# Attention decode kernel: K of the last pair in one load, and `wo` in six loads instead of seven

## The chip, the cores and the metric

The kernel runs on one core of a Trainium2 chip. The metric is the device time of one execution in microseconds (us). The core has four compute engines that matter here: TensorE (PE in the profile, with its weight loads as PEld), VectorE (DVE), ScalarE (ACT) and GpSimd (POOL). SyncE (SP) issues the loads; its queue is called SPq. Each engine runs its own program in order, and the programs meet only at semaphores.

## The reference

One decoding step of attention over a large cache, times a gate from a small MLP:

```python
# x (2,1,512); k_cache, v_cache (2,32,8192,128); wq (512,4096); wo (4096,512), all float32
xn = layernorm(x)
q = heads(xn @ wq)                                  # 2 x 32 heads, 1 query, 128 wide
scores = einsum("bhqd,bhkd->bhqk", q, k_cache) * 128 ** -0.5
o = einsum("bhqk,bhkd->bhqd", softmax(scores), v_cache)
s = merge_heads(o) @ wo
g = silu(mlp(layernorm(xn)))                        # w1, b1, gelu, w2, b2
return x + s * g
```

The two caches are 268 MB each, so nearly all bytes that the kernel reads are K and V, and every one is read once.

## The kernel before, in words

**Tiling.** There are 2 x 32 = 64 heads. A tile is the K (or V) of two heads: partitions 0 to 63 hold one head and 64 to 127 the other, 128 rows of 128 numbers in each partition, 8.4 MB in all. So there are N = 32 K tiles and 32 V tiles, numbered 0 to 31 here (K0 to K31, V0 to V31), and a *pair* is two tiles, K(2i) and K(2i+1). SBUF holds three such tiles: `KBUF[0]` and `KBUF[1]` take the K tiles in turn, and `VB` takes every V tile but the last. V31 goes to `KBUF[0]`, so that `wo` (8.4 MB too, 32 rows of 512 columns in each partition) can go to `VB`. In the profile all three buffers are called `big`.

**VectorE** works on each K tile in two long instructions: a multiplication with the query (`tensor_tensor`, in place) and a sum over the 128 numbers of a row (`tensor_reduce`, into `sc`). Then it takes the maximum (`MX`), waits for TensorE to transpose that, and reduces it to the negative maximum of each head (`nm`). The function is `scores` (line 317). The first 15 pairs run in a hardware loop (line 331); the last pair, K30 and K31, is written out behind the loop (lines 335 to 337). K31 is loaded in two halves on two semaphores, `d_k1` and `d_kl`, and `scores` multiplies and sums one half and then the other.

**TensorE** runs a loop of 31 turns (line 492): `weighted` multiplies the softmax weights `PZ` with a V tile (64 matmul instructions), transposes the result by way of `o`, and frees `VB` (`p_free`); `softmax` transposes the maximum, spreads the bias, and frees the K buffer (`p_k`). Between these it does matmuls of `Q` with `ident` whose results nobody reads (`unread`, line 448): they only keep TensorE occupied. `unread(4, 4)` stands ahead of the wait for the maximum, `unread(4, 2)` ahead of V31, `unread(2)` between the halves of V31, and a few short ones behind it.

**ScalarE** computes the exponentials into `PZ`, and copies TensorE's sums to SBUF.

**The end** (lines 501 to 530): when V31 has been weighted, VectorE spreads the result (`Z`), TensorE sums it, and VectorE divides by the softmax sums, which gives `on`, the attention output. TensorE then multiplies `on` with the 32 rows of `wo`, in order of the rows, and waits for each load of `wo` by its semaphore `d_wo0`, `d_wo1` and so on. Rows 0 to 27 make one sum in bank 1 (`pw`), which ScalarE copies (`wide`, into `o`); rows 28 to 31 and that copy are added up in `acc`; VectorE multiplies with the gate and adds x (`res`), and SyncE stores it.

**The order of the loads.** SyncE issues, in this order: ..., K31 (waits for `p_k` of tile 29), V30 (waits for `p_free` of tile 29), V31 in two halves (waits for `p_k` of tile 30), then all loads of `wo` (wait for `p_free` of tile 30), and after all work the store. The loads of one queue move their data in the order of issue.

Of the kernel before, what the change touches and what calls it, by code (L numbers as in the profile page):

```python
# [5 lines left out]
ALU = mybir.AluOpType  # L6
AX = mybir.AxisListType
# [6 lines left out]
class Program:  # L14
# [28 lines left out]
    def take(self, eng, name, v=1):  # L43

        self.engines[eng].wait_ge(self.sem(name), v).then_inc(self.sem(name), -v)  # L45

    def op(self, eng, method, *args, waits=(), sig=None, by=1, quiet=False, **kwargs):
        need = self.need(eng, waits)
        for name, v in need[:-1]:
            self.engines[eng].wait_ge(self.sem(name), v)  # L50
        ins = getattr(self.engines[eng], method)(*args, **kwargs)  # L51
        for name, v in need[-1:]:
            ins._wait_ge(self.sem(name), v)
        if quiet:
            return None
        name = sig or "own_" + eng
        by = 16 if method == "dma_start" else by
        ins.then_inc(self.sem(name), by)
        self.counts[name] += by
        return name, self.counts[name]  # L60


def decode_kernel(nc, x, kc, vc, wq, wo, w1, b1, w2, b2, out):
    P = 128
    B, H, S, DH = kc.shape
# [3 lines left out]
    U = 2  # L69
    HP = P // U  # L70
    KP = S // HP
    HH = H // U
    N = B * HH
# [13 lines left out]
    OC = DH // PH  # L87
    BH = B * H
    NPB = 512 // DH
    WO_CUTS = (0, 10, 18, 24, 28, 30, 31, 32)  # L90
    WIDE = 28
    HALVES = (0, KP // 2, KP)

    pr = Program(nc)
    op, wait, take = pr.op, pr.wait, pr.take

    def sb(shape, name):
        return nc.alloc_sbuf_tensor(name, list(shape), F32).ap()
# [4 lines left out]
    kf = kc.rearrange("b h s d -> (b h s d)").rearrange("(n p j d) -> n p j d", p=P, j=KP, d=DH)  # L103
# [4 lines left out]
    KBUF, VB = rows[:2], rows[2]  # L108
# [24 lines left out]
    Q = sb([P, N, DH], "Q")  # L133
# [21 lines left out]
    SC = [sb([P, KP], f"sc{i}") for i in range(2)]  # L155
# [36 lines left out]
    def pe_n(name, n):  # L192
        return name, n + 1
# [9 lines left out]
    op("SP", "dma_start", wq_sb, wq.rearrange("(p c) n -> p c n", p=P), sig="d_wq")  # L203

    def load_k(n, *waits):
        sems, cuts = ([f"d_k{n % U}", "d_kl"], HALVES) if n == N - 1 else ([f"d_k{n % U}"], (0, KP))
        for name, (c0, c1) in zip(sems, zip(cuts, cuts[1:])):
            op("SP", "dma_start", KBUF[n % U][:, c0:c1], kf[n][:, c0:c1], sig=name, waits=waits)

    load_k(0)  # L210
    t["w2"] = op("SP", "dma_start", w2_sb[:, :NF, :], w2[:NF * P, :].rearrange("(p c) n -> p c n", p=P), sig="d_w2")

# [13 lines left out]
    for k in (7, 6, 1, 2, 4, 0):  # L226
# [13 lines left out]
                  op=ALU.add)  # L240
    t["sel"] = op("DVE", "tensor_copy",
                  sel[:, HP:].rearrange("p (b j r) -> p b j r", b=B, r=HG)[:, :, :QT, 0], by_row[:, :B, :],
                  waits=[t["sel0"]])
# [36 lines left out]
    for part, n0, n1 in (("first", 0, NPB), ("rest", NPB, N)):  # L280
        shape = [BH, n1 - n0, DH]
        t[f"QN {part}"] = op("DVE", "tensor_tensor", out=QN[:, n0:n1, :], in0=q_all.unsqueeze(1).to_broadcast(shape),
                           in1=mine[:, n0:n1].unsqueeze(2).to_broadcast(shape), op=ALU.mult,
                           waits=[t["qall"], t["mine"]])
# [10 lines left out]


    load_k(1, pe("pq"), ("d_wq", 16))
    for b in range(B):
        t["x4"] = op("SP", "dma_start", x4[HB * b::R, :], x[b, 0].rearrange("(j n) -> j n", n=P), sig="d_x4",
                     waits=[t["x4m"]])  # L300
# [4 lines left out]
    for n in range(N - 2):  # L305
        load_k(n + 2, pe_n("p_k", n))
        op("SP", "dma_start", VB, vf[n + 1], sig="d_v", waits=[pe_n("p_free", n)])
# [4 lines left out]
    wo_v = wo.rearrange("(p c) n -> p c n", p=P)  # L312
    for i, (c0, c1) in enumerate(zip(WO_CUTS, WO_CUTS[1:])):
        op("SP", "dma_start", wo_sb[:, c0:c1], wo_v[:, c0:c1], sig=f"d_wo{i}")


    def scores(u, q, sems, cuts):
        k = KBUF[u]
        for name, (c0, c1) in zip(sems, zip(cuts, cuts[1:])):
            take("DVE", name, 16)  # L320
            op("DVE", "tensor_tensor", out=k[:, c0:c1], in0=k[:, c0:c1],
               in1=q.unsqueeze(1).to_broadcast([P, c1 - c0, DH]), op=ALU.mult, sig="v_t")
            take("DVE", "v_t")
            op("DVE", "tensor_reduce", out=SC[u][:, c0:c1], in_=k[:, c0:c1], axis=AX.X, op=ALU.add, sig="v_r")
        take("DVE", "v_r", len(sems))
        op("DVE", "tensor_reduce", out=MX, in_=SC[u], axis=AX.X, op=ALU.max, sig="v_mx")
        take("DVE", "p_m")
        op("DVE", "tensor_reduce", out=nm, in_=pm[:1, :P].rearrange("o (s r) -> o s r", s=U), axis=AX.X,
           op=ALU.max, negate=True, sig="v_nm")

    with nc.vector.Fori(0, N // U - 1) as i:
        take("DVE", "s_q")
        for u in range(U):
            scores(u, Q.rearrange("p (i u) d -> p i u d", u=U)[:, i, u, :], [f"d_k{u}"], (0, KP))
    take("DVE", "s_q")
    scores(0, Q[:, N - U, :], ["d_k0"], (0, KP))
    scores(1, Q[:, N - 1, :], ["d_k1", "d_kl"], HALVES)


    with nc.scalar.Fori(0, N // U) as i:  # L340
        for u in range(U):
# [4 lines left out]
            for s in range(U):  # L346
# [10 lines left out]
                   waits=[t["th"], t["pool"]])  # L357
    shape = [P, N, U * PH]
    t["ZL"] = op("DVE", "tensor_tensor", out=ZL, in0=half.unsqueeze(1).to_broadcast(shape),
                 in1=RS.unsqueeze(2).to_broadcast(shape), op=ALU.mult, waits=[pe_n("p_z", 0), t["half"]])  # L360
# [3 lines left out]
                in1=OT.unsqueeze(2).to_broadcast(shape), op=ALU.mult, waits=[t["OT"], t["blk"]])  # L364
    t["on"] = op("DVE", "tensor_tensor", out=on[:, ::HB, :], in0=OA[:, :, :OC], in1=rl.unsqueeze(2).to_broadcast([P, B, OC]),
                 op=ALU.mult, waits=[t["rl"], t["on0"], pe_n("p_oa", 0)])
    t["wide"] = op("ACT", "copy", o4, pw, waits=[pe_n("p_w", 0)])
    a = op("DVE", "scalar_tensor_tensor", res, acc, 0.5, gate, op0=ALU.mult, op1=ALU.mult,
           waits=[pe_n("p_acc", 0), t["gate"]])
    t["res"] = op("DVE", "tensor_add", res, res, x4, waits=[a, t["x4"]])  # L370
    t["out"] = op("SP", "dma_start", out.rearrange("b s (j n) -> j (b s) n", n=P), res[::HB, :], sig="d_out",
                  waits=[t["res"]])
# [27 lines left out]
    for c in range(ND):  # L400
# [4 lines left out]
        j, k = NF % QT, NF // QT  # L405
# [6 lines left out]
    j, k = NF % QT, NF // QT  # L412
    mm(ph[R * j:R * j + B, k * P:k * P + FT], ones[:1, :B], b1_sb[:, NF * P:], start=False, stop=True, sig="ph")
    by_tile = ident.rearrange("p (j r) -> p j r", r=R)
    for k in range(NH):
        n = min(QT, NF + 1 - k * QT)
# [9 lines left out]
    for n in range(NG // QT):  # L426
        for hh in range(HG):
# [3 lines left out]
               waits=[t["sel"], t["qnat"]], sig="pqa" if last else None)  # L431

    for g in range(N // NPB):
        mm(PB[g % len(PB)], sides, QN[:, g * NPB:(g + 1) * NPB, :].rearrange("h n d -> h (n d)"),
           waits=[t["side"], t["QN rest" if g else "QN first"]] + ([t[f"Q{QH}"]] if g >= len(PB) else []),
           sig=f"pb{g}")
    for f in range(NF + 1):
        j = f % QT
        k = P if f < NF else FT
        mm(pg[R * j:R * j + B, :], hT[:k, f, :], w2_sb[:k, f, :], start=f < QT, stop=f + QT > NF and j != QT - 1,  # L440
           waits=[t["hT"], t["w2"], t["mem6"]])
    mm(pg[R * (QT - 1):R * (QT - 1) + B, :], ones[:1, :B], b2_sb, start=False, stop=True, waits=[t["b2"]], sig="pg")
    for j in range(QT):
        mm(pgate[R * j:R * j + MB, :], mod_b[:, :MB], g_nat[:, j * P:(j + 1) * P], waits=[t["g"], t["mod_b"]],
           sig="pgate" if j == QT - 1 else None)
    assert done == PE_EVENTS, done

    def unread(*heads):

        for n in heads:  # L450
            mm(bank[6][:, :n * DH], ident, Q[:, :n, :].rearrange("p n d -> p (n d)"), waits=[t["g"], t[f"Q{QH}"]])
# [58 lines left out]
    for b in range(B):  # L510
        h = slice(b * H, (b + 1) * H)
        mm(OA[:, b, :OC], Z[:, h].rearrange("p h r -> p (h r)"), mod, waits=[t["Z"]],
           sig="p_oa" if b == B - 1 else None)
    unread(1)
    for i, (c0, c1) in enumerate(zip(WO_CUTS, WO_CUTS[1:])):
        for c in range(c0, c1):
            after = [t["on"], t["mem"], (f"d_wo{i}", 16)]
            if c < WIDE:
                j = c % QT
                mm(pw[R * j:R * j + MB, :], on[:, :, c], wo_sb[:, c, :], start=c < QT, stop=c + QT >= WIDE,  # L520
                   waits=after, sig="p_w" if c == WIDE - 1 else None)
# [5 lines left out]
        if c1 == OC - 2:  # L527
            for j in range(QT):
                mm(acc[R * j:R * j + MB, :], mod[:, :MB], o4[:, j * P:(j + 1) * P], start=False, stop=False,
                   waits=[t["wide"]])  # L530
# [26 lines left out]
```

## Time and profile before

| what | us |
|---|---|
| median of 3 runs (1299.6 to 1299.94) | 1299.65 |
| span of the profiled execution, first to last instruction | 1298.1 |
| what lies around the span, if that execution took the median | 1.55 |
| TensorE busy in the span | 466.2 |
| VectorE busy in the span | 1135.7 |
| ScalarE busy in the span | 72.0 |
| share of the DMA engines' time taken by the load queue | 99.7% |
| data read | 559.30 MB, 431 GB/s over the span |

The profile is one execution. Its page gives shares of the whole span; its timeline gives the start and the duration of each instruction (or of several alike, merged, with "xN"), and in brackets how long the engine had been idle and what ended that. `DVEq`, `PEq` and `ACTq` there are the engines' own sequencers: an instruction that waited for a semaphore ahead of the work is put down to them. `PEclk` is TensorE's granted clock, 1.00 for full and 0.50 for half.

### The profile page before, as it was taken

The page shows a single profiled execution, that of the slowest core. Times are in us where ns is not written, and L with a number is a line of the kernel's source. Part 1 is how long each engine was busy: PE and PEld are TensorE (multiplying, and loading weights), DVE is VectorE, ACT ScalarE, POOL GpSimd, SP SyncE. Part 2 cuts the span into 40 slices and gives each one's busy share as a digit, 9 for nine tenths or more (in the row PEclk, how much of TensorE's full clock was granted, in tenths as well). Part 3 has the DMA queues.
Part 4 walks back from the last instruction along what each step waited for, and adds up shares of the span by engine and source line. Part 5 has one row for each costly group of instructions (what it writes and reads, how often), then busy time and mean ns, then how long its engine had stood idle before and what let it go on. Part 6 is the DMA issues. An engine that isn't in the chain of part 4 may idle for free. (4 is left out here: it accounts for less than half of the span.)

```text
span 1298.1 us, 7183 instructions
## 1 busy us (share of the span) xinstructions
PE 466.2 (36%) x2958; PEld 151.0 (12%) x2958; DVE 1135.7 (87%) x171; ACT 72.0 (6%) x245; POOL 2.1 (0%) x14
## 2 busy tenths in 40 slices
PE   3813343323334322433322343322334321333338
PEld 1201111001111000111100111100111100111103
DVE  2599999988889988889988888988888988888991
ACT  1100000000000000000000000000000000000000
POOL 0000000000000000000000000000000000000000
PEclk8757766666776566677656767656776666677659
DMA  9999999999999999999999999999999999999998
GB/s 412 432 430 440 432 434 432 426 440 432 438 432 428 436 430 438 434 432 434 426 440 432 436 434 426 438 430 438 434 432 434 426 440 432 434 436 426 426 434 364
DMA packets 11098, 559.38 MB, mean 431 GB/s; under 512 B 1248, under 2 KB 1264, under 8 KB 1748
## 3 DMA queue, kind: packets, MB, share of 16 engines
q1 hardware_dynamic: 11084, 559.30, 99.7%
q8 instruction: 3, 0.05, 0.0%
q14 instruction: 3, 0.02, 0.0%
q10 hardware_dynamic: 8, 0.01, 0.0%
HBM read 559.30 MB, written 0.00 MB: 431 GB/s over the span
## 5 line engine op out<-in xcount | busy, mean ns | idle before, releaser
L51 DVE TENSOR_TENSOR big<-big,Q 128x16384 f32<-128x16384 f32 (+1 forms) x33 | 551.3, 16707 | 72.9 <-DVEq L45 72.9
L51 DVE TENSOR_REDUCE sc<-big 128x128 f32<-128x16384 f32 (+1 forms) x33 | 551.2, 16703 | 4.8
L51 PE MATMUL bank<-big,PZ 128*8 128x512 f32 x2048 | 293.3, 737 | 628.0 <-PEq L45 628.0
L51 PEld LDWEIGHTS bank<-big,PZ 128*8 128x8 f32 x2048 | 60.5, 103 | 833.5 <-issue 833.5
L51 PE MATMUL bank<-Q,ident 128*128 128x512 f32 (+2 forms) x198 | 79.9, 514 | 0.2 <-issue 0.2
L51 ACT COPY o<-bank 128x512 f32<-128x512 f32 x33 | 19.4, 586 | 892.8 <-ACTq L45 881.3
L51 PE MATMUL bank<-ident,MX 128*1 128x128 f32 x32 | 10.0, 313 | 136.1 <-PEq L45 136.1
L51 PE MATMUL bank<-mod,o 128*128 128x2 f32 x256 | 32.8, 250 | 27.4 <-PEq L45 27.4
L51 PEld LDWEIGHTS bank<-mod,o 128*128 128x128 f32 x256 | 31.0, 191 | 55.4 <-issue 55.4
L51 PEld LDWEIGHTS bank<-Q,ident 128*128 128x128 f32 x198 | 35.0, 206 | 16.5 <-issue 16.5
L51 DVE TENSOR_REDUCE nm<-bank 1x2 f32<-1x128 f32 x32 | 8.9, 279 | 19.6 <-DVEq L45 19.6
L51 ACT ACTIVATE PZ<-sc,bias 64x128 f32<-64x128 f32 x64 | 25.5, 399 | 6.6 <-ACTq L45 6.2
L51 DVE TENSOR_TENSOR big<-big,mine 64x512 f32<-64x512 f32 (+1 forms) x2 | 4.5, 2278 | 20.4 <-ACT big L51 20.4
L51 PEld LDWEIGHTS bank<-ident,MX 128*1 128x1 f32 x32 | 2.5, 79 | 161.1 <-issue 161.1
L51 ACT COPY bias<-bank 128x1 f32<-128x1 f32 x32 | 5.1, 159 | 224.2 <-ACTq L45 224.2
L51 PE MATMUL bank<-big,sides 64*128 64x512 f32 x16 | 12.8, 975 | 3.7 <-DVE big L51 3.7
L51 PE MATMUL bank<-nm,srow 1*64 1x1 f32 x128 | 10.6, 221 | 8.9 <-PEq L45 7.3
L51 DVE TENSOR_REDUCE MX<-sc 128x1 f32<-128x128 f32 x32 | 9.2, 286 | 4.7
L51 PE MATMUL bank<-big,xnT 128*2 128x512 f32 x64 | 9.0, 728 | 9.4 <-DMA big<-in_A_wq_dram 9.4
L51 ACT ACTIVATION_READ_ACCUMULATOR PZ<-sc,bias x64 | 11.8, 184 | 0.0
L51 PE MATMUL bank<-big,on 128*17 128x512 f32 (+1 forms) x88 | 10.7, 569 | 1.1 <-DMA big<-in_A_wo_dram 0.8
L51 DVE SCALAR_TENSOR_TENSOR res<-bank,gate 128x128 f32<-128x128 f32 x1 | 0.3, 293 | 11.9 <-PE bank L51 11.9
(78 smaller groups left out, 74.6 us busy)
## 6 DMA issues: line engine op xcount, KB each, us to landing
big<-in_A_k_cache_dram SPq DMA_DIRECT2D x2, 4096.0 KB, 35.8
big<-in_A_v_cache_dram SPq DMA_DIRECT2D x2, 4096.0 KB, 35.9
big<-in_B_w_dram SPq DMA_DIRECT2D x1, 2752.0 KB, 10.1
big<-in_B_w_dram SPq DMA_DIRECT2D x1, 2560.0 KB, 51.6
big<-in_A_wo_dram SPq DMA_DIRECT2D x1, 2560.0 KB, 15.0
big<-in_A_wo_dram SPq DMA_DIRECT2D x1, 2048.0 KB, 19.6
big<-in_A_wo_dram SPq DMA_DIRECT2D x1, 1536.0 KB, 22.8
big<-in_A_wo_dram SPq DMA_DIRECT2D x1, 1024.0 KB, 24.4
```

What stands on the lines that cost most here:

```text
L51: ins = getattr(self.engines[eng], method)(*args, **kwargs)
```

## The change

K31 is loaded in one piece like every other K tile, on `d_k1` alone. With that, the last pair no longer differs from the others, so VectorE's loop runs over all 16 pairs and the code behind it goes; `scores` loses its lists of semaphores and cuts. `wo` comes in six loads of 16, 8, 4, 2, 1 and 1 rows, where it was seven of 10, 8, 6, 4, 2, 1 and 1.

```diff
-    WO_CUTS = (0, 10, 18, 24, 28, 30, 31, 32)
+    WO_CUTS = (0, 16, 24, 28, 30, 31, 32)
...
     def load_k(n, *waits):
-        sems, cuts = ([f"d_k{n % U}", "d_kl"], HALVES) if n == N - 1 else ([f"d_k{n % U}"], (0, KP))
-        for name, (c0, c1) in zip(sems, zip(cuts, cuts[1:])):
-            op("SP", "dma_start", KBUF[n % U][:, c0:c1], kf[n][:, c0:c1], sig=name, waits=waits)
+        op("SP", "dma_start", KBUF[n % U], kf[n], sig=f"d_k{n % U}", waits=waits)
...
-    def scores(u, q, sems, cuts):
+    def scores(u, q):
         k = KBUF[u]
-        for name, (c0, c1) in zip(sems, zip(cuts, cuts[1:])):
-            take("DVE", name, 16)
-            op("DVE", "tensor_tensor", out=k[:, c0:c1], in0=k[:, c0:c1],
-               in1=q.unsqueeze(1).to_broadcast([P, c1 - c0, DH]), op=ALU.mult, sig="v_t")
-            take("DVE", "v_t")
-            op("DVE", "tensor_reduce", out=SC[u][:, c0:c1], in_=k[:, c0:c1], axis=AX.X, op=ALU.add, sig="v_r")
-        take("DVE", "v_r", len(sems))
+        take("DVE", f"d_k{u}", 16)
+        op("DVE", "tensor_tensor", out=k, in0=k, in1=q.unsqueeze(1).to_broadcast([P, KP, DH]), op=ALU.mult, sig="v_t")
+        take("DVE", "v_t")
+        op("DVE", "tensor_reduce", out=SC[u], in_=k, axis=AX.X, op=ALU.add, sig="v_r")
+        take("DVE", "v_r")
...
-    with nc.vector.Fori(0, N // U - 1) as i:
+    with nc.vector.Fori(0, N // U) as i:
         take("DVE", "s_q")
         for u in range(U):
-            scores(u, Q.rearrange("p (i u) d -> p i u d", u=U)[:, i, u, :], [f"d_k{u}"], (0, KP))
-    take("DVE", "s_q")
-    scores(0, Q[:, N - U, :], ["d_k0"], (0, KP))
-    scores(1, Q[:, N - 1, :], ["d_k1", "d_kl"], HALVES)
+            scores(u, Q.rearrange("p (i u) d -> p i u d", u=U)[:, i, u, :])
```

On VectorE, what stood behind the loop's branch before was the last pair (`big0` is K30, `big1` K31, each wait in brackets):

```order
L331 COMPARE_AND_BRANCH
L51 TENSOR_TENSOR big0<-big0,Q 128x16384 [waits s_q,d_k0]
L51 TENSOR_REDUCE sc0<-big0 128x128 [waits v_t]
L51 TENSOR_REDUCE MX<-sc0 128x1 [waits v_r]
L51 TENSOR_REDUCE nm<-bank1 1x2 [waits p_m]
L51 TENSOR_TENSOR big1<-big1,Q 128x8192 [waits d_k1]
L51 TENSOR_REDUCE sc1<-big1 128x64 [waits v_t]
L51 TENSOR_TENSOR big1<-big1,Q 128x8192 [waits d_kl]
L51 TENSOR_REDUCE sc1<-big1 128x64 [waits v_t]
L51 TENSOR_REDUCE MX<-sc1 128x1 [waits v_r]
L51 TENSOR_REDUCE nm<-bank1 1x2 [waits p_m]
L51 SCALAR_TENSOR_TENSOR gate<-th,z 128x128 [waits own_ACT]
```

After the change the second tile of the loop's body serves K31 too, and the work of the end follows the branch directly:

```order
L51 ISA [waits d_k1]
L51 TENSOR_TENSOR big1<-big1,Q 128x16384
L51 TENSOR_REDUCE sc1<-big1 128x128 [waits v_t]
L51 TENSOR_REDUCE MX<-sc1 128x1 [waits v_r]
L51 TENSOR_REDUCE nm<-bank1 1x2 [waits p_m]
L327 REGISTER_ALU
L327 COMPARE_AND_BRANCH
L51 SCALAR_TENSOR_TENSOR gate<-th,z 128x128 [waits own_ACT]
L51 TENSOR_TENSOR ZL<-half,RS 128x256 [waits p_z]
```

So K31's multiplication now waits for all of K31 instead of for its first half, and nothing else has changed places on VectorE.

On SyncE's queue the end of the order of loads changes as follows (K31, V30, V31, `wo`):

```order
-L51 DMA big<-in_A_k_cache_dram 128x8192 [waits p_k]
-L51 DMA big<-in_A_k_cache_dram 128x8192
+L51 DMA big<-in_A_k_cache_dram 128x16384 [waits p_k]
 L51 DMA big<-in_A_v_cache_dram 128x16384 [waits p_free]
 L51 DMA big<-in_A_v_cache_dram 128x8192 [waits p_k]
 L51 DMA big<-in_A_v_cache_dram 128x8192
-L51 DMA big<-in_A_wo_dram 128x5120 [waits p_free]
+L51 DMA big<-in_A_wo_dram 128x8192 [waits p_free]
 L51 DMA big<-in_A_wo_dram 128x4096
-L51 DMA big<-in_A_wo_dram 128x3072
```

The sequence and the waits stay; two issues fewer are made, and the same bytes come in the same order.

## Prediction, made before the run

> **What bounds the kernel now.** I read the page's head and its chain first, then the timeline of the last 130 us, then TensorE's clock in slices. The page with its list of DMA issues, and below it the last load in the chain in order of time (start, duration), say:
>
> ```profile
> span 1298.1 us, 7183 instructions
> q1 hardware_dynamic: 11084, 559.30, 99.7%
> HBM read 559.30 MB, written 0.00 MB: 431 GB/s over the span
> DMA big<-in_A_wo_dram 2%; SPq L51 0%; PE bank L51 0%; DVE res L51 0%; DVEq L50 0%
> big<-in_A_wo_dram SPq DMA_DIRECT2D x1, 2560.0 KB, 15.0
> big<-in_A_wo_dram SPq DMA_DIRECT2D x1, 2048.0 KB, 19.6
> ```
>
> ```profile
> 1269.47 25.60 DMA big<-in_A_wo_dram
> ```
>
> The loads are never idle, and the chain that ends last is the last load of `wo`, which lands at 1295.07. No compute engine bounds the kernel as a whole. The change touches no byte of the stream, so it can only act at the two ends of the stream's last 60 us: on when a consumer starts, and on whether a consumer is still behind when the last row of `wo` lands. The question is how much slack each has. VectorE around the last three K tiles, and TensorE's start on V29 and V30 (timeline: start, duration, and idle time ahead in brackets):
>
> ```profile
> 1159.37 17.23 DVE L51 TENSOR_TENSOR big<-big,Q 128x16384 f32<-128x16384 f32 x1 [2.82 <-DVEq L45]
> 1197.97 17.23 DVE L51 TENSOR_TENSOR big<-big,Q 128x16384 f32<-128x16384 f32 x1 [2.74 <-DVEq L45]
> 1215.34 17.22 DVE L51 TENSOR_REDUCE sc<-big 128x128 f32<-128x16384 f32 x1
> 1217.33 9.68 PE L51 MATMUL bank<-big,PZ 128*8 128x512 f32 x64 [21.58 <-PEq L45]
> 1232.71 0.29 DVE L51 TENSOR_REDUCE MX<-sc 128x1 f32<-128x128 f32 x1
> 1233.87 8.67 DVE L51 TENSOR_TENSOR big<-big,Q 128x8192 f32<-128x8192 f32 x1
> 1242.69 8.69 DVE L51 TENSOR_REDUCE sc<-big 128x64 f32<-128x8192 f32 x1
> 1251.29 8.68 DVE L51 TENSOR_TENSOR big<-big,Q 128x8192 f32<-128x8192 f32 x1
> 1256.09 9.08 PE L51 MATMUL bank<-big,PZ 128*8 128x512 f32 x64 [21.62 <-PEq L45]
> 1260.12 8.69 DVE L51 TENSOR_REDUCE sc<-big 128x64 f32<-128x8192 f32 x1
> 1268.95 0.29 DVE L51 TENSOR_REDUCE MX<-sc 128x1 f32<-128x128 f32 x1
> ```
>
> In the steady loop VectorE waits some 2.8 us for each K tile: K29 began at 1159.37 and K30 at 1197.97, 38.6 us apart, with V29 (1217.33) and V30 (1256.09) 38.76 apart. K31 alone began without a wait, 35.9 us after K30, since its first half had landed while K30 was being worked on. From there VectorE ran through: four half instructions back to back until the maximum at 1268.95. Now the end:
>
> ```profile
> 1266.43 3.47 SPq L51 DMA_DIRECT2D big<-in_A_wo_dram  x7
> 1266.93 1.96 PE L51 MATMUL bank<-Q,ident 128*128 128x512 f32 x4
> 1269.38 0.27 PE L51 MATMUL bank<-ident,MX 128*1 128x128 f32 x1 [0.48 <-PEq L45]
> 1270.73 1.56 PE L51 MATMUL bank<-Q,ident 128*128 128x512 f32 x4 [0.22 <-issue]
> 1272.22 3.62 PE L51 MATMUL bank<-big,PZ 128*8 128x512 f32 x32
> 1276.40 3.62 PE L51 MATMUL bank<-big,PZ 128*8 128x512 f32 x32
> 1283.46 0.23 DVE L51 TENSOR_TENSOR on<-bank,rl 128x64 f32<-128x64 f32 x1 [0.72 <-PE bank L51]
> 1283.83 8.21 PE L51 MATMUL bank<-big,on 128*17 128x512 f32 x48
> 1292.61 1.09 PE L51 MATMUL bank<-big,on 128*17 128x512 f32 x8 [0.57 <-DMA big<-in_A_wo_dram]
> 1293.75 0.60 ACT L51 COPY o<-bank 128x512 f32<-128x512 f32 x1 [11.47 <-PE bank L51]
> 1295.12 0.19 PEld L51 LDWEIGHTS bank<-big,on 128*17 128x17 f32 x8 [0.35 <-DMA big<-in_A_wo_dram]
> 1295.62 0.29 DVE L51 SCALAR_TENSOR_TENSOR res<-bank,gate 128x128 f32<-128x128 f32 x1 [11.94 <-PE bank L51]
> ```
>
> TensorE reached `wo` at 1283.83, worked through rows 0 to 23 (48 instructions), then waited for loads: for rows 24 to 27 until 1292.61, and for row 31, 0.35 us, until 1295.12. Since `wo` arrives more slowly than TensorE eats it, a late start of TensorE is made up until that slack is gone.
>
> **The change, part by part.**
>
> *K31 in one load.* K31's multiplication now starts when the whole tile has landed. By the 38.6 and 38.76 us steps that is 1236.57 to 1236.73; midway between the starts of V29 and V30 is 1236.71. I take 1236.67, 2.80 us later than 1233.87. From a start to the maximum a whole tile takes 34.74 us (K30: 1197.97 to 1232.71), the two halves took 35.08 (1233.87 to 1268.95). So the maximum comes at 1271.41, **2.46 us late**, and everything that hangs on it moves by as much at an equal clock: TensorE's transpose, the exponentials, V31 (to 1274.7; both halves of V31 have landed by 1276.40 even before), `on` (end 1283.69 to 1286.15), row 0 of `wo` (1283.83 to 1286.3).
>
> *Waits behind it.* Queued behind VectorE's wait is only K31's own work. Issues on SyncE's queue don't hang on K31: V31 waits for K30's bias, `wo` for V30's weighting, and K31's maximum is asked for after both. So the stream keeps its times, and the last row still lands at about 1295.07.
>
> *The loop.* The 16th turn replaces straight code. Between K29 and K30, where the loop ended before, VectorE idled 2.74 us against 2.82 a tile earlier, so falling out of the loop cost at most what that wait hid: 0 to 2.74 us. It now falls between `nm` of K31 and the work of the end, whose first piece that anyone waits for is needed only after V31's matmuls, over 7 us later (two of 3.62); that covers it. I take 0, the row's own reading.
>
> *Two loads fewer of K31 and `wo`.* V29 to V30, the step that has K31's extra cut in it, is 0.16 us longer than K29 to K30. So one cut is worth 0 to 0.16 us, two 0 to 0.3; SyncE's seven issues take 3.47 us, about 0.5 each, all hidden behind V31. I take −0.1.
>
> *The first load of `wo` has 16 rows.* The first two issues of the seven ended near 1266.8 and 1267.3, so row 9 landed about 1281.8 (15.0 later) and row 17 about 1286.9 (19.6 later); between them row 15 about 1285.6. TensorE gets there at 1286.3, so this wait costs nothing; the cover is 0.7 us, and without K31's delay the part alone would hold TensorE from 1283.83 to 1285.6. Rows 16 to 31 are there at the same times as before.
>
> *TensorE catching up.* At full clock 16 tiles of V31 take 3.62 us, 0.226 each, and rows of `wo` are matmuls of the same 512 columns: 28 rows are 6.3 us, 1286.3 to 1292.6, just when rows 24 to 27 used to begin. No loss then. But the clock matters:
>
> ```profile
> core 0: us, PE busy (x), PEclk, DMA share, GB/s
> 1229.49:1232.91 3.42, 1.25 (x3) 1.00 1.02 441
> 1232.91:1236.32 3.41, 1.18 (x7) 0.50 1.25 538
> 1215.84:1219.25 3.41, 1.92 (x12) 0.50 1.03 442
> 1219.25:1222.67 3.42, 3.42 (x20) 0.50 0.98 422
> 1222.67:1226.08 3.41, 3.41 (x36) 1.00 0.98 423
> 1267.04:1270.45 3.41, 2.57 (x12) 1.00 1.03 442
> 1284.11:1287.52 3.41, 3.41 (x20) 0.50 0.98 414
> ```
>
> The clock changes only at steps of 3.41 us. A slice with 1.25 us of TensorE's work was followed by half clock; one with 2.57 was not. At half clock a slice with 1.92 us of work did not bring the full clock back, a full one did. A slice at half clock loses up to 1.7 us of work. Such a slice lay on `wo` before, 1284.11 to 1287.52, and was absorbed. If it recurs, rows 0 to 27 end at 1294.3 instead of 1293.70 (1292.61 + 1.09); the copy and what follows move by 0.6, of which the 0.35 us wait for row 31 swallows a part: +0.25.
>
> New is TensorE's gap ahead of the late maximum: `unread(4, 4)` ends at 1268.89 and the transpose comes at 1271.84 (1269.38 + 2.46), so the gap grows from 0.48 to 2.95 us. With the short matmuls behind it, `unread(4, 2)` starts at 1273.2: 4.3 us with under 1 us of work. A slice that lies in it looks like the one at 1229.49, and half clock then falls on V31. How much depends on where the 3.41 us steps lie, which one profile can't tell for other executions. One slice partly on V31: 0 to 1.7 us of loss, 0.85 midway.
>
> [...]
>
> *The sum.* Late start absorbed, 0; the old half-clock slice again on `wo`, 0 to +0.25; a slice on V31, 0 to +1.7, midway +0.85, which costs in full only if the slack is gone, so I count +0.6; cuts −0.1. Together about **+0.7 us**. On the span of 1298.1 that is 1298.8, and with the 1.55 us around the span that the median implies, **1300.35 us**.
>
> **The rivals.**
>
> *The clock stays up.* If the quiet stretch straddles two slices so that both hold enough work, or such a gap doesn't count, V31 runs at full clock and the last load ends the kernel as before: 1299.55 to 1299.9. For it: the slice at 1267.04 with 2.57 us of work kept its clock. Against it: 4.3 us of quiet is longer than a slice.
>
> *Slower by over 0.2%: two slices at half clock.* If the quiet slice ends in mid-gap, the next one is half filled with waiting, like 1215.84 to 1219.25, and does not bring the full clock back; V31 loses up to 2 x 1.7 us. It decides once V31 loses more than about 2.4 us: then `wo` starts near 1289 and its own slice has nothing left to hide in. +0.25 + 2.4 to 3.4, or **1302.3 to 1303.3**. Against it: it needs a certain position of the steps and a second slice that stays low.
>
> *The change doesn't do what it says, with gain.* If the stream is shortened by fewer cuts and nothing is late, the end moves by −0.1 to −0.3: 1299.35 to 1299.55. The loads being busy 99.7%, more isn't to be had; a gain of 2.6 us is excluded by every row here, short of a mechanism that I don't see.
>
> **How the numbers follow.** 0.2% of 1299.65 is 2.6 us, about what a measurement of this kernel can tell from no change. Forecast (one slice, +0.25 to +2.0): 0.42. Clock stays up: 0.25. Two slices: 0.27, nearly all beyond 2.6 us in a median that falls there. Stream shorter: 0.04. Something unseen: 0.02. That gives faster 0.03, same 0.70, slower 0.27. The range runs from the shorter stream, 1299.4, to the top of the two-slice case, 1303.2; the likeliest case's own range is 1299.9 to 1301.7.
>
> **What would show it.** In the profile after: K31's multiplication starting near 1236.7 with a wait of about 2.8 us; one instruction of 17.2 us in place of two halves; the maximum near 1271.4; TensorE's gap ahead of it near 2.9 us; row 0 of `wo` between 1286.3 and 1289; the clock in the slices from 1270 to 1280. If TensorE no longer waits for rows 28 to 31, the end hangs on VectorE's chain. I am wrong if the last row of `wo` lands elsewhere than 1295 ± 0.4, if VectorE stalls on leaving the loop for over 7 us, or if K31 lands late for a reason not in these rows.

## The result, and the profile after

The changed kernel takes 1302.59 us (median of 20 executions, 1299.57 to 1303.94); the kernel before takes 1299.88 us beside it (20 executions, 1299.48 to 1300.91). The ratio is 1.0018, 95% interval [1.0012, 1.0024]: slower by some 2.3 us, between 1.6 and 3.1; the two medians alone lie 2.7 us apart. The single times are as telling as the median: before, all 20 lie within 1.4 us; after, within 4.4 us, and the fastest is as fast as before.

The page of the changed kernel's profiled execution, span and chain:

```profile
span 1301.4 us, 7182 instructions
PE 1%; DVE 0%; ACT 0%; issue 0%; ACTq 0%; DVEq 0%
```

The chain that ends last no longer holds a load. It is TensorE now, followed back through ScalarE's and VectorE's small steps. The timeline of that execution, from K30's sum and K31's multiplication to the last step:

```profile
1215.68 17.22 DVE L51 TENSOR_REDUCE sc<-big 128x128 f32<-128x16384 f32 x1
1237.02 17.23 DVE L51 TENSOR_TENSOR big<-big,Q 128x16384 f32<-128x16384 f32 x1 [2.83 <-DVEq L45]
1256.28 9.97 PE L51 MATMUL bank<-big,PZ 128*8 128x512 f32 x64 [21.67 <-PEq L45]
1271.76 0.29 DVE L51 TENSOR_REDUCE MX<-sc 128x1 f32<-128x128 f32 x1
1272.19 0.27 PE L51 MATMUL bank<-ident,MX 128*1 128x128 f32 x1 [2.21 <-PEq L45]
1272.61 0.28 DVE L51 TENSOR_REDUCE nm<-bank 1x2 f32<-1x128 f32 x1 [0.57 <-DVEq L45]
1272.82 0.28 DVE L51 SCALAR_TENSOR_TENSOR gate<-th,z 128x128 f32<-128x128 f32 x1
1273.54 2.93 PE L51 MATMUL bank<-Q,ident 128*128 128x512 f32 x4
1276.40 5.02 PE L51 MATMUL bank<-big,PZ 128*8 128x512 f32 x32
1281.97 3.62 PE L51 MATMUL bank<-big,PZ 128*8 128x512 f32 x32
1289.03 0.23 DVE L51 TENSOR_TENSOR on<-bank,rl 128x64 f32<-128x64 f32 x1 [0.72 <-PE bank L51]
1289.40 8.37 PE L51 MATMUL bank<-big,on 128*17 128x512 f32 x72
1297.40 0.58 ACT L51 COPY o<-bank 128x512 f32<-128x512 f32 x1 [9.55 <-PE bank L51]
1298.95 0.29 DVE L51 SCALAR_TENSOR_TENSOR res<-bank,gate 128x128 f32<-128x128 f32 x1 [9.70 <-PE bank L51]
```

Read against the rows of before, the lateness grows in three steps and shrinks in two:

| at | before | after | late by |
|---|---|---|---|
| K31's maximum | 1268.95 | 1271.76 | 2.81 |
| first matmul of V31 | 1272.22 | 1276.40 | 4.18 |
| second half of V31 | 1276.40 | 1281.97 | 5.57 |
| `on` | 1283.46 | 1289.03 | 5.57 |
| `wide` | 1293.75 | 1297.40 | 3.65 |
| `res` | 1295.62 | 1298.95 | 3.33 |

K31's multiplication starts 3.15 us later than before (1237.02 against 1233.87), since VectorE waited 2.83 us for the whole tile; from there to the maximum it takes 34.74 us instead of 35.08. So the maximum is 2.81 us late. Of these, 0.34 aren't K31's: in this execution K30's sum already began at 1215.68 instead of 1215.34. The next 1.37 are the `unread(4, 2)` matmuls ahead of V31, which took 2.93 us instead of 1.56. The next 1.39 are the first half of V31, 5.02 us instead of 3.62. Then 2.24 us are won back on `wo` and the steps behind it, since TensorE now does all rows without a wait for any load: all the slack there was in this execution. TensorE's clock in the slices between its steps (columns: the slice, its length, TensorE's busy time and instructions, granted clock, share of the DMA engines, GB/s):

```profile
core 0: us, PE busy (x), PEclk, DMA share, GB/s
1269.03:1272.44 3.41, 1.20 (x6) 1.00 0.96 413
1272.44:1275.86 3.42, 3.04 (x11) 0.50 0.95 405
1275.86:1279.27 3.41, 3.41 (x18) 0.50 1.04 444
1279.27:1282.68 3.41, 3.41 (x30) 1.00 1.07 461
1286.10:1289.51 3.41, 2.97 (x23) 1.00 0.97 411
1289.51:1292.92 3.41, 3.41 (x20) 0.50 0.99 399
1292.92:1296.34 3.42, 3.42 (x39) 1.00 0.24 89
```

The slices follow the steps at which this trace's clock changes: it does so 70 times up to 1292.92, and 68 times up to 1287.52 in the trace of before, each time a whole multiple of 3.413 us after the change ahead of it, to 0.01 us. The slice with the gap ahead of the maximum held 1.20 us of work; two slices at half clock follow, on the unread matmuls and on V31, and a third falls on `wo`, as one did before the change (1284.11 to 1287.52). What brings that third slice isn't explained by these rows: the slice ahead of it held 2.97 us of busy time, before the change too, and yet half clock followed. The row of before:

```profile
1280.69:1284.11 3.42, 2.97 (x22) 1.00 1.01 431
```

In the last slice shown of the changed kernel the loads are over (89 GB/s) and TensorE is still at `wo`.

### The profile page after: what moved, and what is told of

It reads as the page before. It is cut to its first block, busy times and chain, and to the rows that moved or that the text cites. A ratio compares the mean times of both kernels' runs of the same rounds, so it can differ in the third digit from the quotient of the medians.

```text
span 1301.4 us, 7182 instructions
## 1 busy us (share of the span) xinstructions
PE 462.3 (36%) x2958; PEld 150.5 (12%) x2958; DVE 1135.6 (87%) x169; ACT 71.9 (6%) x245; POOL 2.1 (0%) x14
## 5 line engine op out<-in xcount | busy, mean ns | idle before, releaser
L51 DVE TENSOR_TENSOR big<-big,Q 128x16384 f32<-128x16384 f32 x32 | 551.2, 17225 | 75.3 <-DVEq L45 75.3
L51 DVE TENSOR_REDUCE sc<-big 128x128 f32<-128x16384 f32 x32 | 551.0, 17220 | 4.7
L51 PE MATMUL bank<-big,PZ 128*8 128x512 f32 x2048 | 289.3, 728 | 628.3 <-PEq L45 628.3
L51 PEld LDWEIGHTS bank<-nm,srow 1*64 1x64 f32 x128 | 8.8, 169 | 16.1 <-issue 16.1
```

## The experiments

Theory A puts together the pieces that the prediction names: K31's late start makes TensorE late and quiet, the quiet slice brings half clock, and the two together use up the slack of `wo`. Theory B: the bigger first load of `wo` holds TensorE back. Theory C: leaving the loop late stalls VectorE. Theory A2: lateness alone does it, the clock is beside the point. Each ratio is against runs of the kernel before on the same chip.

| run | what it is | median us | ratio, 95% interval |
|---|---|---|---|
| changed kernel | | 1302.59 | 1.0018 [1.0012, 1.0024] |
| e1_wo_six | `wo` in six loads alone | 1300.02 | 1.0000 [0.9991, 1.0009] |
| e2_k_whole | K31 in one load alone | 1302.80 | 1.0018 [1.0009, 1.0027] |
| e3_loop_halves | loop, every second tile in two loads | 1300.94 | 1.0009 [1.0000, 1.0018] |
| e4_busy | changed kernel, gap filled with matmuls | 1300.21 | 1.0004 [0.9995, 1.0013] |
| e5_no_filler | changed kernel, no unread matmuls ahead of V31 | 1301.57 | 1.0012 [1.0003, 1.0021] |
| e6_quiet_before | kernel before, gap made quiet | 1300.01 | 1.0002 [0.9992, 1.0011] |
| e7_loop_prefilled | loop, K31 alone in two loads | 1299.78 | 0.9997 [0.9988, 1.0006] |

### Which part of the change: `wo` or K31

Run e1_wo_six is the kernel before with one line changed:

```diff
-    WO_CUTS = (0, 10, 18, 24, 28, 30, 31, 32)
+    WO_CUTS = (0, 16, 24, 28, 30, 31, 32)
```

> Half of the change alone: wo in six loads (16, 8, 4, 2, 1, 1 rows), with K31 in two halves and VectorE's last pair written out as before. Theory A (K31's late start lets TensorE's clock fall on V31): the maximum of K31 stays near 1269, row 0 of wo waits for the 16-row load until about 1285.6 instead of starting at 1283.8, and catches up: 0 to +0.5 us, about 1300.0. Theory B (the bigger first load of wo holds TensorE back): most of the +2.7 us, about 1302.5. Theory C (leaving the loop late stalls VectorE): no loss, 1299.9.

Measured: 1300.02 us (1299.63 to 1300.95), no difference. Its timeline, TensorE on rows 0 to 29 of `wo` (72 instructions) and the copy of the sum of rows 0 to 27:

```profile
1285.44 9.32 PE L51 MATMUL bank<-big,on 128*17 128x512 f32 x72 [1.52 <-DMA big<-in_A_wo_dram]
1294.28 0.59 ACT L51 COPY o<-bank 128x512 f32<-128x512 f32 x1 [11.81 <-PE bank L51]
```

TensorE did wait for the 16 rows, until 1285.44 (the prediction's part on that load said 1285.6), with 1.52 us of idle time. That was absorbed: the copy came 0.53 us later than before (1294.28 against 1293.75), and the kernel's time is the same. Theory B is out.

Run e2_k_whole is the kernel before with K31 in one load and the pair behind the loop left written out:

```diff
-        sems, cuts = ([f"d_k{n % U}", "d_kl"], HALVES) if n == N - 1 else ([f"d_k{n % U}"], (0, KP))
+        sems, cuts = [f"d_k{n % U}"], (0, KP)
...
-    scores(1, Q[:, N - 1, :], ["d_k1", "d_kl"], HALVES)
+    scores(1, Q[:, N - 1, :], ["d_k1"], (0, KP))
```

> The other half alone, without the loop: K31 in one load, the last pair still written out behind a loop of 15 turns, wo in seven loads. Theory A: the whole loss, +2.0 to +3.0 us (about 1302.4), with a wait of 2.8 us ahead of K31's multiplication. Theory B: no loss, 1299.9. Theory C: no loss beyond the late start itself, which wo's slack absorbs: 1299.9 to 1300.3.

Measured: 1302.80 us, the whole loss, without the loop and without the change of `wo`. Theory C is out as the cause. The changed kernel's own timeline says the same: the first instruction behind the loop, `gate`, starts at 1272.82, 0.21 us after `nm` (1272.61) began, as close as 0.21 us before (1269.81 and 1270.02).

The eleven times run from 1299.54 to 1303.14, eight of them 1302.3 or more. The profiled one was the fastest of them, 1299.54 (span 1298.2). Its timeline and its clock show the same late K31 without the loss:

```profile
1271.62 0.29 DVE L51 TENSOR_REDUCE MX<-sc 128x1 f32<-128x128 f32 x1
1272.06 0.27 PE L51 MATMUL bank<-ident,MX 128*1 128x128 f32 x1 [3.52 <-PEq L45]
1273.44 2.93 PE L51 MATMUL bank<-Q,ident 128*128 128x512 f32 x4 [0.20 <-issue]
1276.30 3.64 PE L51 MATMUL bank<-big,PZ 128*8 128x512 f32 x32
1287.55 0.23 DVE L51 TENSOR_TENSOR on<-bank,rl 128x64 f32<-128x64 f32 x1 [0.72 <-PE bank L51]
1287.93 6.78 PE L51 MATMUL bank<-big,on 128*17 128x512 f32 x72
```

```profile
core 0: us, PE busy (x), PEclk, DMA share, GB/s
1269.57:1272.99 3.42, 0.58 (x6) 1.00 1.02 434
1272.99:1276.40 3.41, 3.21 (x12) 0.50 0.91 388
1276.40:1279.81 3.41, 3.41 (x32) 1.00 1.01 432
1286.64:1290.05 3.41, 3.06 (x26) 1.00 0.98 411
```

Here the 3.41 us steps lay 0.54 us later than in the changed kernel's profile. Half clock followed the quiet slice (0.58 us of work) here too, but only for one slice, which ended at 1276.40, just as V31 began (1276.30); V31's first half took 3.64 us, `wo` ran at full clock from the start (6.78 us for rows 0 to 29, against 8.37), and nearly all of it fitted into the slack: `on` was 4.09 us later than before, `res` 0.16 (1295.78 against 1295.62). So two programs in which K31 is equally late end with or without a loss by where the clock's steps fall. That the steps also make the difference between the eleven times of this one program is argued from these two traces; none of its executions with the loss was traced.

### Whether K31's halves are what matters, and what a cut costs

Run e3_loop_halves keeps the loop over all pairs and the six loads of `wo`, and gives every second tile two loads (`scores` takes its lists of semaphores and cuts again, as before the change):

```diff
-    def load_k(n, *waits):
-        op("SP", "dma_start", KBUF[n % U], kf[n], sig=f"d_k{n % U}", waits=waits)
+    def load_k(n, *waits):
+        sems, cuts = ([f"d_k{n % U}", "d_kl"], HALVES) if n % U else ([f"d_k{n % U}"], (0, KP))
+        for name, (c0, c1) in zip(sems, zip(cuts, cuts[1:])):
+            op("SP", "dma_start", KBUF[n % U][:, c0:c1], kf[n][:, c0:c1], sig=name, waits=waits)
...
-            scores(u, Q.rearrange("p (i u) d -> p i u d", u=U)[:, i, u, :])
+            scores(u, Q.rearrange("p (i u) d -> p i u d", u=U)[:, i, u, :], *((["d_k1", "d_kl"], HALVES) if u else (["d_k0"], (0, KP))))
```

> One loop over all 16 pairs as after the change, wo in six loads, but the second K tile of every pair comes in two halves on two semaphores, so that K31's first half can be worked on early. Theory A: K31 starts near 1234 again and the loss goes: 1299.8 to 1300.5 (15 more cuts cost the stream 0 to 1 us, if one costs anything). Theory B and C: the loss stays, about 1302.5.

Measured: 1300.94 us (1300.69 to 1301.97): most of the loss is gone, and 0.9 us more than e1_wo_six stays. Run e7_loop_prefilled asks where that comes from. It works on the same halves in the same loop, but cuts only K31; the second semaphore is filled once with what the 15 earlier turns take from it:

```diff
-        sems, cuts = ([f"d_k{n % U}", "d_kl"], HALVES) if n % U else ([f"d_k{n % U}"], (0, KP))
+        sems, cuts = ([f"d_k{n % U}", "d_kl"], HALVES) if n == N - 1 else ([f"d_k{n % U}"], (0, KP))
...
     op("DVE", "memset", eps_t, EPS)
+    nc.vector.nop().then_inc(pr.sem("d_kl"), 16 * (N // U - 1))
```

> One loop over all pairs and wo in six loads, as after the change, but every second tile is worked on in two halves, and only K31 is loaded in two halves: the second half's semaphore is filled at the start with 15 turns' worth, so that the earlier turns pass through it. No extra cuts of the stream. Theory A: the loss goes altogether, 1299.8 to 1300.2, and K31 starts near 1234. If the loop's exit cost something: 1300.5 or more. If the 15 extra cuts were not what the run with halves in every pair paid, it would be near that run's 1300.9.

Measured: 1299.78 us (1299.53 to 1301.02), level with the kernel before, with one loop over all pairs. The first half of K31, and `on`, first in e3_loop_halves and then in e7_loop_prefilled:

```profile
1235.26 8.69 DVE L51 TENSOR_TENSOR big<-big,Q 128x8192 f32<-128x8192 f32 x1
1257.47 8.62 PE L51 MATMUL bank<-big,PZ 128*8 128x512 f32 x64 [21.75 <-PEq L45]
1285.02 0.22 DVE L51 TENSOR_TENSOR on<-bank,rl 128x64 f32<-128x64 f32 x1 [0.85 <-PE bank L51]
```

```profile
1234.07 8.69 DVE L51 TENSOR_TENSOR big<-big,Q 128x8192 f32<-128x8192 f32 x1
1256.28 8.38 PE L51 MATMUL bank<-big,PZ 128*8 128x512 f32 x64 [21.74 <-PEq L45]
1283.68 0.23 DVE L51 TENSOR_TENSOR on<-bank,rl 128x64 f32<-128x64 f32 x1 [0.72 <-PE bank L51]
```

Both start K31 early. With 15 more cuts TensorE starts on V30 1.19 us later (1257.47 against 1256.28), so by these two executions a cut in this stream costs about 0.08 us; that accounts for e3's remainder. (Without the extra cuts this start lies between 1256.09 and 1256.39 in the profiles here, so 1.1 to 1.4 us for 15 cuts.) And neither the loop nor its exit costs anything that can be measured.

### Lateness or clock

Run e4_busy is the changed kernel with TensorE's gap partly filled (the call stands in all turns):

```diff
-            unread(4, 4)
+            unread(4, 4, 4, 4)
```

> The changed kernel with four more unread matmuls of 512 columns ahead of the wait for the maximum (two calls of unread more), which fill some 1.7 us of TensorE's gap ahead of K31's maximum; K31 is as late as after the change. Theory A with the clock as the amplifier: the slice ahead of V31 keeps full clock in most executions, V31 starts near 1275 at full clock, and the median falls to 1300.0 to 1301.5. Theory A2 (lateness alone, the clock is beside the point): no change against the changed kernel, about 1302.6.

Measured: 1300.21 us (1299.64 to 1303.41). Its timeline and clock:

```profile
1271.66 0.29 DVE L51 TENSOR_REDUCE MX<-sc 128x1 f32<-128x128 f32 x1
1272.09 0.27 PE L51 MATMUL bank<-ident,MX 128*1 128x128 f32 x1 [0.89 <-PEq L45]
1274.93 3.62 PE L51 MATMUL bank<-big,PZ 128*8 128x512 f32 x32
1286.17 0.23 DVE L51 TENSOR_TENSOR on<-bank,rl 128x64 f32<-128x64 f32 x1 [0.72 <-PE bank L51]
1286.54 5.51 PE L51 MATMUL bank<-big,on 128*17 128x512 f32 x48
1292.61 1.09 PE L51 MATMUL bank<-big,on 128*17 128x512 f32 x8 [0.55 <-DMA big<-in_A_wo_dram]
```

```profile
core 0: us, PE busy (x), PEclk, DMA share, GB/s
1268.13:1271.54 3.41, 3.07 (x8) 1.00 0.98 423
1271.54:1274.96 3.42, 2.29 (x15) 1.00 0.97 414
```

The maximum is as late as in the changed kernel (1271.66), but the gap is 0.89 us instead of 2.21, no slice falls under 2.29 us of work, and the clock stays up. `on` comes 2.71 us late, just K31's delay, and TensorE has caught up by rows 24 to 27, for which it waits until 1292.61 as it did before. No half-clock slice fell on `wo` in this execution either. So the lateness alone is absorbed, and A2 is out. Of the eleven times one is 1303.41 and two more are 1301.19 and 1301.46: the filling makes the loss rarer, it doesn't exclude it.

Run e6_quiet_before asks the reverse. It is the kernel before, not late, but without the unread matmuls ahead of the maximum, in all turns:

```diff
-        if not first:
-            unread(4, 4)
         take("PE", "v_mx")
```

> The kernel before, without the unread matmuls ahead of the wait for the maximum (the call with 4 and 4 heads, in all turns): TensorE is quiet ahead of K31's maximum as after the change, but K31 is not late. It tells what the clock costs without the lateness. Theory A: V31 runs partly at half clock, on comes 1.5 to 3 us later than 1283.7, and the slack of wo's stream absorbs nearly all: 1299.8 to 1300.8. If half clock alone made the loss, 1302 or more.

Measured: 1300.01 us (1299.68 to 1301.34). The timeline shows the same two stretched steps as in the changed kernel, unread matmuls and first half of V31:

```profile
1269.59 0.27 PE L51 MATMUL bank<-ident,MX 128*1 128x128 f32 x1 [2.70 <-PEq L45]
1270.93 2.93 PE L51 MATMUL bank<-Q,ident 128*128 128x512 f32 x4
1273.79 5.03 PE L51 MATMUL bank<-big,PZ 128*8 128x512 f32 x32
1286.44 0.23 DVE L51 TENSOR_TENSOR on<-bank,rl 128x64 f32<-128x64 f32 x1 [0.72 <-PE bank L51]
```

Here too a quiet slice (0.71 us of work in 3.41) was followed by two at half clock, the first with 3.02 us of work. The maximum is only 0.20 us late (1269.15 against 1268.95), `on` 2.98, so half clock alone makes 2.78. This execution ends 0.74 us late (`res` at 1296.36, span 1298.8), but the median is level with before. So neither lateness nor clock moves the median by itself. Together they were 5.57 us (2.81 + 2.76) in the changed kernel's profile.

How much of a delay is won back depends on the clock on `wo`. The profiles, each against that of before:

| profile | `on` late by | `res` late by | won back | clock at the start of `wo` |
|---|---|---|---|---|
| changed kernel | 5.57 | 3.33 | 2.24 | half |
| e6_quiet_before | 2.98 | 0.74 | 2.24 | half |
| e2_k_whole | 4.09 | 0.16 | 3.93 | full |
| e5_no_filler (below) | 4.96 | 1.03 | 3.93 | full |

In these profiles the slack is thus 2.24 us with a half-clock slice on `wo` and 3.93 us without one. The difference, 1.69 us, is about half of a slice of 3.41. By this estimate the slice on `wo` makes about half of the 3.33 us by which the changed kernel's profiled execution ends late: at full clock there, 5.57 - 3.93 = 1.64 would be left.

Run e5_no_filler leaves out of the changed kernel the unread matmuls ahead of V31:

```diff
-        if last:
-            unread(4, 2)
         take("PE", "s_pz")
```

> The changed kernel without the unread matmuls ahead of V31 (the call with 4 and 2 heads). In the changed kernel's profile these took 2.93 us at half clock and V31 began at 1276.4, 1.5 us after its weights were ready (1274.9). Theory A (K31 late, and half clock on what TensorE does next): V31 begins near 1275.1, part of its matmuls still run at half clock; about half of the loss goes: 1301.0 to 1302.2. If the filler were no part of the loss: 1302.6. If the filler were all of it: 1299.9.

Measured: 1301.57 us (1300.40 to 1302.68). V31 and `on`:

```profile
1275.13 5.68 PE L51 MATMUL bank<-big,PZ 128*8 128x512 f32 x32 [1.61 <-PEq L45]
1288.42 0.23 DVE L51 TENSOR_TENSOR on<-bank,rl 128x64 f32<-128x64 f32 x1 [0.72 <-PE bank L51]
```

V31 begins at 1275.13 instead of 1276.40, at half clock (5.68 us for its first half). By the medians about two fifths of the loss go, 1.0 of 2.7 us, and the slowest time falls from 1303.94 to 1302.68; the intervals of the two ratios overlap, so the size of this gain is uncertain. In the traces the matmuls that keep TensorE occupied are themselves in the way at half clock: V31 starts 1.27 us earlier without them. The fastest time rises, from 1299.57 to 1300.40. The profiled execution is that fastest one, and it shows half clock all the same: by its timeline, cut back in steps of 3.41 us from the change of clock near 1279.36, the quiet slice (1269.12 to 1272.53) held 1.18 us of work, the next one only 1.58 us without the filler, and the clock stayed at half until 1279.36. That the fastest executions of the changed kernel escape this because of the filler is argued; none of them was traced.

## Why the prediction was right or wrong

- **The place and the kind, right.** K31's multiplication was to start near 1236.7 with a wait of 2.8 us, and did at 1237.02 with 2.83; the maximum near 1271.4 came at 1271.76, 34.74 us behind its start as the sum had it. K31's own delay is the 2.46 us forecast (2.47); the rest is that K30 was already 0.34 us later. One instruction of 17.23 us replaced two halves.
- **The stream unchanged, right.** V30's matmuls begin within 0.2 us of before in the changed kernel (1256.28), and no bytes of `wo` move after 1295; a cut, bounded at 0 to 0.16 us, measured about 0.08.
- **`wo`'s first load and the loop, right:** both cost nothing, the first because the wait until 1285.44 is absorbed (e1_wo_six), the second by `gate`'s row and e7_loop_prefilled.
- **Lateness absorbed at full clock, right** (e4_busy: row 0 at 1286.54 and no loss).
- **Three signs missed.** TensorE's gap was to be near 2.9 us and was 2.21, since V30's matmuls took 9.97 us instead of 9.08 (half clock lasted until 1262.21 instead of 1260.21) and the unread matmuls behind them ended later; the clock fell all the same. Row 0 of `wo` came at 1289.40, later than the 1286.3 to 1289 given. The end hung on TensorE's work on `wo` rather than on VectorE's chain.
- **The size, wrong.** The forecast was 1300.35 us, "one slice", with its own range of 1299.9 to 1301.7; the median is 1302.59, inside the stated range and inside the rival of two slices (1302.3 to 1303.3), which had 0.27. The term that failed is "a slice on V31, 0 to +1.7, midway +0.85". It counted V31's own stretch only. The unread matmuls ahead of V31 stretch as well, 1.37 us, and V31 queues behind them. With V31's 1.39 the clock's part measured 2.76 us. One slice alone measured 1.42 us (e2_k_whole: `on` 4.09 late, K31's maximum 2.67), nearly all of it on the unread matmuls (2.93 us instead of 1.56). The term "the old half-clock slice again on `wo`, 0 to +0.25" was too small as well once the slack was gone: 1.69 us by the table of slack. What the rival of two slices described is what the changed kernel's profile shows: a second, partly filled slice at half clock, `wo` starting beyond 1289, and "its own slice" with "nothing left to hide in". Its sum, +2.65 to +3.65 us, holds the 3.33 of that execution.
- **Its chance, wrong.** "It needs a certain position of the steps and a second slice that stays low" was put as unlikely. Of the 31 times of the two kernels that load K31 in one piece (the changed one and e2_k_whole), 4 lie below 1300.35, 5 between 1301.2 and 1302.0, and 22 above 1302.0. By these times the second slice probably stays low more often than I allowed for. Only one execution with the loss was traced, and the middle group needs no second slice: one slice with a half-clock slice on `wo` would leave 4.09 - 2.24 = 1.85 us, an estimate from the table of slack. The slices at half clock that were traced: one with 3.04 us of work in 3.42 (after the change) and one with 3.02 in 3.41 (e6_quiet_before) were followed by another, one with 3.21 in 3.41 (e2_k_whole) by full clock. The row of before that I judged by held 1.92 us, far less than any of these.
- **The clock.** Gaps of 2.21 us (changed kernel) and 2.70 us (e6_quiet_before) ahead of the maximum were followed by half clock, where their slices held 1.20 and 0.71 us of work. Slices with 2.29 us (e4_busy) and 2.57 us (before) were followed by full clock. Busy time alone doesn't sort all rows, though: the slice with 2.97 us ahead of `wo` was followed by half clock, before the change and after, and the prediction didn't weigh that row. Why stays open.
- **The sign.** The 0.70 for "within 0.2%" holds by the ratio, 1.0018, though only just; by its interval the kernel is slower.

## What to carry to other kernels

A consumer that is faster than the last load hides its own lateness until that slack is gone, so add the delays up before setting them against the slack: here 2.7 us of late start alone (e4_busy) and 2.8 us of half clock alone (e6_quiet_before) left the median where it was, and both together raised it by some 2.3 us. The slack itself depended on the clock, 3.93 or 2.24 us. A wait that is lengthened ahead of TensorE can cost more than its length if the clock falls on the work behind it, as it did here (2.83 us of wait ahead of K31, `on` 5.57 us late in the same trace), and how much depends on where the steps lie in each execution: look at single times, not only at a median. A tile that is split only at the end of a program can still be handled in one loop if its second semaphore is filled beforehand.

## What the runs showed of the hardware that was not expected

One profile can miss a loss altogether: the profiled execution of e2_k_whole was the fastest of eleven and had a span of 1298.2 us, like the kernel before, while its median was 1302.80. And matmuls that only keep TensorE occupied took 2.93 us instead of 1.56 once the clock had fallen, so that V31 started 1.27 us earlier without them and the median was 1.0 us lower (e5_no_filler), though the intervals of the two ratios overlap. The slice of `wo` at half clock cost nothing before the change and, by the table of slack, about 1.7 us once the slack was gone.
